# Two-block decode attention: K and V of block B in 32 KB rows per partition, two slots each, P^T spread by TensorE

## The chip, the cores and the metric

The kernel runs on one core of a Trainium2 chip. The metric is device time in microseconds (us), the median of repeated executions. Engines are called PE (TensorE), PEld (its weight loads), DVE (VectorE), ACT (ScalarE), POOL (GpSimd) and SP (SyncE, which here issues nearly all DMAs). Sixteen DMA engines move the data.

## The reference

Two blocks, A and B, do the same thing for one new token and are concatenated. A looks at the last 2048 cached positions, B at all 8192.

```python
# x: (1, 1, 576); k_cache, v_cache: (1, 16 heads, 8192, 128); wq: (576, 4096); wo: (4096, 576); bf16
q = (x @ wq).reshape(B, Sq, 32, 128).transpose(0, 2, 1, 3)
k = jnp.repeat(k_cache, 2, axis=1)      # A: positions Sk - 2048 .. Sk only
v = jnp.repeat(v_cache, 2, axis=1)
scores = jnp.einsum("bhqd,bhkd->bhqk", q, k) * (128 ** -0.5)
p = softmax(scores)
o = jnp.einsum("bhqk,bhkd->bhqd", p, v)
out = o.transpose(0, 2, 1, 3).reshape(B, Sq, 4096) @ wo
# result: concatenate([A's out, B's out])
```

Each K and V head of B is 8192 x 128 x 2 bytes = 2 MB, of A's window 0.5 MB. With wq and wo of both blocks 102.8 MB have to come from HBM once, and every byte is used for little arithmetic.

## The kernel before, in words

**Tiling.** K and V are loaded in groups of 8 MB: one group for A (all 16 heads, 2048 positions) and four for B (8 heads and 4096 positions each; groups 1 and 2 are the first 4096 positions, groups 3 and 4 the last). A group lies in four slots of 2 MB: `kslots` and `vslots` have NS = 4 slots of 8192 bf16 per partition. One load fills one slot: a partition receives TS = 64 consecutive positions of one head, one contiguous row of 16 KB; a slot holds four heads of A or two heads of B (`load_kv`, from L387). wq comes in pieces of 4, 4 and 1 units of 2048 columns (16, 16 and 4 KB per partition) into slots that K or V need later; wo comes in nine pieces.

**K rounds** (g = 0 to 4). PE transposes a slot's 64 blocks of 128x128 into PSUM in two units (`k_transpose`, L466; a unit is 4 banks of 8 blocks). Per unit ACT copies banks 0 and 2 to SBUF (L472) and DVE banks 1 and 3 (L475), into one of four `kt` buffers. `k_scores` (L486) multiplies the transposed unit with the queries of the slot's heads (`qst`, which POOL copies from `qtm`, L457) into the score tile `sacc`, 128x1024 in two PSUM banks. The stationary operand is zero in all rows but those of its heads, so units of all heads add into one tile, and the tile must be zero beforehand (`scores_zero`, L497, by PE).

**Softmax.** After rounds 0, 2 and 4 a chunk of scores is complete (A; B's first and second half). DVE masks (A only, L514) and takes the maximum (L515), ACT takes the exponential into `psb` (L523), writing each value twice. In the next odd round PE transposes `psb` (16 blocks, L536) and DVE writes it with a mask per parity of heads into `ptm` (L545, four operations).

**V.** At the end of rounds 1, 3, 4, 5 and 6 PE multiplies `ptm` with the four V slots of a group (`v_slot`, L557, 64 matmuls per slot) into `opsum`; DVE picks the valid part of each row (`v_keep`, L566 and L373). Round 6 also has the softmax weights of both blocks (`weights`, `combine`). Then come wo of A and of B (L646), a cast (L652) and a store (L658) each.

**What sets the order.** The program is a list of operations per engine, in order; `Program` derives semaphore waits from what each reads and writes. PE runs its rounds in a loop: an inner part (transposes, scores, in odd rounds P^T) and an outer part (V). Places in the loop are the numbers given as `loop=`. SP issues loads in the order of the list. It waits before a load until the last reader of the slot is done: PE's transposes for K slots, PE's V products for V slots. All loads of SP run on one queue, q1, first in first out.

Of the kernel before, what the change touches and what calls it, by code (L numbers as in the profile page):

```python
# [16 lines left out]
SLOT = 8192  # L17
UNIT = 4096
NS = 4
NKT = 4  # L20
TS = 64
WQ_UNITS = 9
WQ_U = 2048
OUTW = DM // 4
NEG = -1.0e30
# [13 lines left out]
class Program:  # L39
# [15 lines left out]
    def add(self, eng, fn, reads=(), writes=(), dma=None, after=(), tag=None, inc=1, loop=None):  # L55
        op = Op(eng, fn, tuple(reads), tuple(writes), dma, tag, 16 if dma is not None else inc, loop)
# [77 lines left out]
    def waits_of_loop(self, ops):  # L134
# [9 lines left out]
        for key, places in points.items():  # L144
# [26 lines left out]
            if len(fixed) == len(places):  # L171
                for place, hi in fixed.items():
# [4 lines left out]
                   for n in (1, 2, 16) for first in (0, n) if fits(first, n, some, taker)]  # L177
# [92 lines left out]
def bass_concat_heads__sliding_block_cached__gqa_block_cached__decode_kernel(  # L270
# [22 lines left out]
    G = [4, 2]  # L293
    CHUNK = [0, 1, 1, 2, 2]
    KIND = [0, 1, 2, 1, 2]
    base = [SK - W_A, 0]

# [3 lines left out]
    kslots = nc.alloc_sbuf_tensor("kslots", [128, NS, SLOT], BF16)  # L301
    vslots = nc.alloc_sbuf_tensor("vslots", [128, NS, SLOT], BF16)
    kt = nc.alloc_sbuf_tensor("kt", [128, NKT, UNIT], BF16)
    ptm = nc.alloc_sbuf_tensor("ptm", [128, 2048], BF16)
    psb = nc.alloc_sbuf_tensor("psb", [128, 2048], BF16)
# [6 lines left out]
    zero = nc.alloc_sbuf_tensor("zero", [128, 512], BF16)  # L312
    qtm = nc.alloc_sbuf_tensor("qtm", [128, 3 * 256], BF16)
    qst = nc.alloc_sbuf_tensor("qst", [128, NS * 64], BF16)
    xtwo = nc.alloc_sbuf_tensor("xtwo", [128, 2, 8], BF16)
    xpad = nc.alloc_sbuf_tensor("xpad", [128, 2, 10, 32], BF16)
    par2 = nc.alloc_sbuf_tensor("par2", [128, 2], F32)
    rows = nc.alloc_sbuf_tensor("rows", [128, 3, NS], F32)
# [4 lines left out]
    diag = nc.alloc_sbuf_tensor("diag", [128, 2, DH, NS], F32)  # L323
    acc = nc.alloc_sbuf_tensor("acc", [128, 7, DH], F32)
# [26 lines left out]
    def setup(pool):  # L351
        for t in (ident, xpad, selq, zero, warm, qtm, identf, same, pick):
            pool.memset(t[:], 0.0)
        pool.memset(onesf[:], 1.0)
        return pool.memset(opj[:], 0.0)

    add("pool", setup, writes=["ident", ("xpad", 0), ("xpad", 1), "selq", "ones", "warm", "zero", "identf", "pick", "same",
                               ("qtm", 0), ("qtm", 1), ("qtm", 2), ("opj", 0), ("opj", 1)])
# [9 lines left out]
    add("pool", select(identf[:], 0, [[-1, 128]], 1), reads=["identf"], writes=["identf"])  # L368
    for j in range(4):
        add("pool", select(pick[:], -128 * j, [[1, 4], [-1, 128]], 4), reads=["pick"], writes=["pick"])  # L370
# [8 lines left out]
    def load(dst, src, writes, dma, after=()):  # L379
        add("sp", lambda sp: sp.dma_start(dst, src()), writes=writes, dma=dma, after=after)  # L380

    def load_wq(P, k, dst, n, res):
        lo = 4 * k * WQ_U
        load(dst, lambda: wqs[P].rearrange("(m r) n -> m (r n)", m=64)
             .rearrange("m (e y) -> (m e) y", e=2)[:, lo:lo + n * WQ_U], [res], "wq%d%d" % (P, k))

    def load_kv(arrs, g, s, slots, name, after=()):  # L387
        P = 0 if g == 0 else 1
        i = s if g == 0 else 4 * ((g - 1) % 2) + s
        ch = 128 // G[P] * TS  # L390
        r0 = base[P] + (0 if g == 0 else (g - 1) // 2 * ch)

        def src():
            return arrs[P][0, i * G[P]:(i + 1) * G[P], r0:r0 + ch, :].rearrange("g (p t) d -> p g (t d)", t=TS)
        load(slots[:, s, :], src, [(name, s)], "%s%d" % (name, s), after)
# [3 lines left out]
    ODD = lambda g: (g & 1) == 1  # L399
    V_OF = {1: 0, 3: 1, 4: 2, 5: 3, 6: 4}  # L400
# [4 lines left out]
    prog.rounds_of, prog.outer = rounds_of, len(V_OF)  # L405
# [11 lines left out]
    def q_part(P, k, n, src, res):  # L417
        def mm(pe):
            for u in range(4 * k, 4 * k + n):
                for c in range(2):  # L420
                    for j in range(4):
                        n_ = 2 * j + c
                        x = u // 2 if n_ // 4 == u % 2 else 5 + (u + 1) // 2
                        o = (u - 4 * k) * WQ_U + (n_ % 4) * 512
                        ins = pe.matmul(qps[c][32 * j:32 * j + 32, :], lhsT=xpad[:, P, x, :],  # L425
                                        rhs=src[:, o:o + 512], start=(u == 0), stop=(u == WQ_UNITS - 1))
            return ins
        add("pe", mm, reads=[("xpad", P), res], writes=qbank)

    def q_finish(P):  # L430
# [12 lines left out]

        def put(dve):
            for e in range(2):
                if P == 0:
                    dst = bass.AP(tensor=qtm, offset=e, ap=[[768, 128], [4, 2], [34, 2], [72, 4]])
                else:
                    dst = bass.AP(tensor=qtm, offset=256 + e, ap=[[768, 128], [68, 2], [34, 2], [136, 4]])
                src = opsum[:, 0:32].rearrange("p (b a e j) -> p b a e j", b=2, a=2, e=2)[:, :, :, e, :]  # L450
                ins = dve.tensor_copy(dst, src)
            return ins
        add("dve", put, reads=[B_O], writes=[("qtm", 0)] if P == 0 else [("qtm", 1), ("qtm", 2)])

    def q_stage(g, s):
        o = KIND[g] * 256 + s * 64
        add("pool", lambda pool: pool.tensor_copy(qst[:, s * 64:(s + 1) * 64], qtm[:, o:o + 64]),  # L457
            reads=[("qtm", KIND[g])], writes=[("qst", s)], tag="q%d" % s)

    def k_transpose(g, u, place):  # L460
        s, half = divmod(u, 2)
        for q in range(4):
            def tr(pe, q=q):
                for t in range(8):
                    o = (32 * half + 8 * q + t) * 128
                    ins = pe.matmul(ktps_bf[q][:, t * 128:(t + 1) * 128], lhsT=kslots[:, s, o:o + 128],  # L466
                                    rhs=ident[:, :], start=True, stop=True, is_transpose=True)
                return ins
            add("pe", tr, reads=[("k", s), "ident"], writes=[("bank", q)], loop=(g, place + q / 8, K_ON, "inner"))
            dst = kt[:, u % NKT, q * 1024:(q + 1) * 1024]  # L470
# [8 lines left out]
    def k_scores(g, u, place):  # L479
        s, half = divmod(u, 2)  # L480

        def mm(pe):
            for e in range(2):
                for j in range(4):
                    rhs = kt[:, u % NKT, j * 1024:(j + 1) * 1024].rearrange("d (x g) -> d x g", g=2)[:, :, e]
                    ins = pe.matmul(sacc[32 * j:32 * j + 32, 512 * half:512 * half + 512],  # L486
                                    lhsT=qst[:, s * 64 + e * 32:s * 64 + e * 32 + 32],
                                    rhs=rhs, start=False, stop=True, skip_group_check=True)
            return ins
        add("pe", mm, reads=[("qst", s)] + [("kt", u % NKT, q) for q in range(4)], writes=[B_S[half]],  # L490
            loop=(g, place, K_ON, "inner"))

    def scores_zero(loop):
        for h in range(2):
            def mm(pe, h=h):
                for j in range(4):
                    ins = pe.matmul(sacc[32 * j:32 * j + 32, 512 * h:512 * h + 512], lhsT=zero[:, 0:32], rhs=zero[:, :],  # L497
                                    start=True, stop=True, skip_group_check=True)
                return ins
            add("pe", mm, reads=["zero"], writes=[B_S[h]], loop=loop and (loop[0], loop[1] + h / 8) + loop[2:])  # L500
# [7 lines left out]
    def softmax_exp(c):  # L508
        P, k = (0, 0) if c == 0 else (1, c - 1)
        if P == 0:  # L510

            v = sacc[:, :].rearrange("p (x b) -> p x b", b=2)
            m = bass.AP(tensor=maskS, offset=2, ap=[[4, 128], [0, 512], [1, 2]])
# [4 lines left out]
            reads=[("st", P, C_M + k)], writes=[("st", P, C_NB + k)])  # L518


        def go(act):
            src = bass.AP(tensor=sacc, offset=0, ap=[[1024, 128], [1, 1024], [0, 2]])
            return act.activation(psb[:, :].rearrange("p (x g) -> p x g", g=2), src, ACT.Exp, bias=st(P, C_NB + k),  # L523
                                  scale=SCALE, accum_out=st(P, C_L + k))
        add("act", go, reads=B_S + [("st", P, C_NB + k)], writes=["psb", ("st", P, C_L + k)], tag="exp")


    def softmax_transpose(g, place):
        for u in range(2):
            dst = (misc if u == 0 else opsum)[:, :].bitcast(BF16)  # L530
            bank = B_M if u == 0 else B_O

            def tr(pe, u=u, dst=dst):
                for t in range(8):
                    o = (8 * u + t) * 128
                    ins = pe.matmul(dst[:, t * 128:(t + 1) * 128], lhsT=psb[:, o:o + 128], rhs=ident[:, :],  # L536
                                    start=True, stop=True, is_transpose=True)
                return ins
            add("pe", tr, reads=["psb", "ident"], writes=[bank], loop=(g, place + u / 8, ODD, "inner"))

            def put(dve, u=u, dst=dst):
                for e in range(2):
                    to = ptm[:, u * 1024:(u + 1) * 1024].rearrange("p (n e y) -> p n e y", e=2, y=2)[:, :, e, :]
                    src = dst.rearrange("p (n e y) -> p n e y", e=2, y=2)[:, :, e, :]
                    ins = dve.tensor_scalar(to, src, par2[:, e:e + 1], None, ALU.mult)  # L545
                return ins
            add("dve", put, reads=[bank, "par2"], writes=[("ptm", u)], tag="put%d" % u, inc=1 if g == 1 else 2)


    def v_slot(vg, s, place, g):  # L550
        def mm(pe):
            for u in range(2):
                for t in range(8):
                    for j in range(4):
                        b = 32 * u + 8 * j + t
                        o = (u * 32 + t * 4 + j) * 32
# [199 lines left out]
```

## Time and profile before

| What | Value |
|---|---|
| median of three runs | 250.0 us (249.79 to 250.01) |
| profiled execution, its own time | 249.46 us |
| its span | 247.7 us |
| mean granted TensorE clock | 0.82 |
| bytes on SP's queue | 102.77 MB |
| steady rate, 30 to 220 us | 428 GB/s |
| ACT / DVE copies of K (L472 / L475) | 77.9 / 55.2 us |
| PE transposes of K (L466) | 85.1 us |
| V products (L557) | 28.1 us |

The profile gives, for each engine, busy time and share of the span; a table of 40 slices of the span with busy tenths of each engine, the TensorE clock that was granted, the DMA engines' busy share and their rate; the DMA queues with packets and bytes; the chain of work that ended last; groups of instructions by line with shapes, count, mean duration, and what ended the idle time before them. The trace behind it has every instruction, DMA packet (start, duration, size) and landing of a DMA (sixteen semaphore updates, one per DMA engine). "First" and "last landing" below are the first and the sixteenth of these.

### The profile page before, as it was taken

Reading aid. Unit: us, or ns where it says so; the run is one execution under the profiler, and the core shown is the slowest. Engines: PE = TensorE matmul, PEld = TensorE weight load, DVE = VectorE, ACT = ScalarE, POOL = GpSimd, SP = SyncE. Lnnn points to the kernel's source line nnn. Section 1 sums busy time; section 2 is a strip of 40 time slices with the busy share of each in tenths; the row PEclk is TensorE's granted clock in tenths of the full one; section 3 lists DMA queues with packets and bytes.
Section 4 is the critical chain, followed back from the end, with each engine's and each line's share of the span. In section 5 each row is a group of like instructions: output and inputs, shape, how many; then the busy total and the mean of one; then the engine's idle time right before and its main releaser. Section 6 shows DMA issues by size and latency. Waiting matters only on the chain. (4 is left out here: it accounts for less than half of the span.)

```text
span 247.7 us, 7505 instructions
## 1 busy us (share of the span) xinstructions
PE 169.6 (68%) x3406; PEld 132.3 (53%) x3406; DVE 81.0 (33%) x152; ACT 87.1 (35%) x92; POOL 12.9 (5%) x49
## 2 busy tenths in 40 slices
PE   0193589994999559995999638998345144685634
PEld 0031288763877458864878428785244142584522
DVE  0001225554555017564555122655004004204000
ACT  2000047767478009786578004775200000000000
POOL 7501000000000000000000000000000000000000
PEclk9999959999799979998899955999858755557555
DMA  7999999999999999999999999999999999999993
GB/s 270 406 433 431 430 431 421 426 423 429 431 425 429 426 421 431 422 431 434 423 429 429 423 431 429 426 437 426 429 429 423 431 426 429 434 427 427 421 406 138
DMA packets 8235, 102.92 MB, mean 416 GB/s; under 512 B 1184, under 2 KB 1312, under 8 KB 2080
## 3 DMA queue, kind: packets, MB, share of 16 engines
q1 hardware_dynamic: 7936, 102.77, 98.0%
q8 instruction: 8, 0.13, 0.2%
q10 hardware_dynamic: 288, 0.00, 0.1%
q14 instruction: 3, 0.02, 0.0%
HBM read 102.76 MB, written 0.00 MB: 415 GB/s over the span
## 5 line engine op out<-in xcount | busy, mean ns | idle before, releaser
L472 ACT ACTIVATE kt<-ktps 128x1024 bf16<-128x1024 bf16 x80 | 77.9, 1021 | 54.5 <-PE ktps L466 54.4
L466 PEld LDWEIGHTS ktps<-ident,kslots 128*128 128x128 bf16 x1280 | 78.9, 103 | 27.9 <-issue 27.9
L466 PE MATMUL ktps<-ident,kslots 128*128 128x128 bf16 x1280 | 85.1, 230 | 12.4 <-PEq L214 12.4
L475 DVE COPY kt<-ktps 128x1024 bf16<-128x1024 bf16 x80 | 55.2, 691 | 53.7 <-PE ktps L466 53.6
L557 PE MATMUL opsum<-vslots,ptm 128*32 128x128 bf16 x1280 | 28.1, 262 | 28.0 <-PEq L214 23.7
L557 PEld LDWEIGHTS opsum<-vslots,ptm 128*32 128x32 bf16 x1280 | 25.3, 119 | 31.6 <-issue 31.6
L486 PE MATMUL sacc<-kt,qst 128*32 128x512 bf16 x320 | 25.3, 392 | 1.8 <-PEq L214 1.8
L566 DVE TENSOR_TENSOR diag<-opsum,rows 128x512 f32<-128x512 f32 x5 | 3.5, 691 | 55.9 <-PE opsum L557 55.9
L425 PE MATMUL opsum<-vslots,xpad 128*32 128x512 bf16 x64 | 8.2, 489 | 14.8 <-DVE xpad L410 12.1
L599 ACT ACTIVATE stat<-stat 128x1 f32<-128x1 f32 (+1 forms) x2 | 0.6, 294 | 37.2 <-DVE stat L597 37.2
L425 PEld LDWEIGHTS opsum<-vslots,xpad 128*32 128x32 bf16 x64 | 2.3, 119 | 17.6 <-issue 13.1
L457 POOL COPY qst<-qtm 128x64 bf16<-128x64 bf16 x20 | 4.5, 236 | 123.2 <-PE sacc L486 113.5
L646 PE MATMUL ktps<-kslots,opj 128*32 128x144 bf16 x184 | 6.1, 326 | 5.8 <-DMA kslots<-in_B_wo_dram 3.9
L486 PEld LDWEIGHTS sacc<-kt,qst 128*32 128x32 bf16 x320 | 5.1, 94 | 8.2 <-issue 4.4
L431 ACT ACTIVATE qrow<-opsum 128x512 bf16<-128x512 f32 x2 | 1.2, 597 | 23.1 <-PE misc L425 23.1
L523 ACT ACTIVATE psb<-sacc,stat 128x2048 bf16<-128x2048 f32 x3 | 5.9, 1967 | 8.5 <-DVE stat L517 8.5
L646 PEld LDWEIGHTS ktps<-kslots,opj 128*32 128x32 bf16 x184 | 5.2, 145 | 6.4 <-DMA kslots<-in_B_wo_dram 4.2
L425 PE MATMUL misc<-vslots,xpad 128*32 128x512 bf16 x64 | 8.2, 487 | 0.0
L630 PE MATMUL misc<-acc,pick 128*128 128x32 f32 x16 | 3.8, 404 | 3.6 <-DVE acc L624 2.9
L433 DVE CAST qrow<-misc 128x512 bf16<-128x512 f32 x2 | 1.4, 692 | 14.6 <-PE misc L425 14.6
L652 DVE CAST outsb<-ktps 128x144 bf16<-128x144 f32 x2 | 0.6, 307 | 16.0 <-PE ktps L646 16.0
L630 PEld LDWEIGHTS misc<-acc,pick 128*128 128x128 f32 x16 | 3.6, 328 | 3.8 <-DVE acc L624 3.0
(66 smaller groups left out, 62.1 us busy)
## 6 DMA issues: line engine op xcount, KB each, us to landing
kslots<-in_B_k_cache_dram SPq DMA_DIRECT2D x16, 2048.0 KB, 19.6
vslots<-in_B_v_cache_dram SPq DMA_DIRECT2D x16, 2048.0 KB, 18.4
kslots<-in_A_k_cache_dram SPq DMA_DIRECT2D x4, 2048.0 KB, 29.8
vslots<-in_A_v_cache_dram SPq DMA_DIRECT2D x4, 2048.0 KB, 23.5
vslots<-in_A_wq_dram SPq DMA_DIRECT2D x2, 2048.0 KB, 9.9
vslots<-in_B_wq_dram SPq DMA_DIRECT2D x2, 2048.0 KB, 19.6
kslots<-in_A_wo_dram SPq DMA_DIRECT2D x2, 2016.0 KB, 23.8
kslots<-in_B_wo_dram SPq DMA_DIRECT2D x1, 2016.0 KB, 31.2
```

The costliest lines, as they stand in the source:

```text
L425: ins = pe.matmul(qps[c][32 * j:32 * j + 32, :], lhsT=xpad[:, P, x, :], rhs=src[:, o:o + 512], start=(u == 0), stop=(u == WQ_UNITS - 1))
L433: add("dve", lambda dve: dve.tensor_copy(qrow[:, 512:1024], misc[:, :]), reads=[B_M], writes=[("qrow", 1)])
L457: add("pool", lambda pool: pool.tensor_copy(qst[:, s * 64:(s + 1) * 64], qtm[:, o:o + 64]), reads=[("qtm", KIND[g])], writes=[("qst", s)], ...
L466: ins = pe.matmul(ktps_bf[q][:, t * 128:(t + 1) * 128], lhsT=kslots[:, s, o:o + 128], rhs=ident[:, :], start=True, stop=True, is_transpose ...
L472: add("act", lambda act, q=q, dst=dst: act.activation(dst, ktps_bf[q], ACT.Copy), reads=[("bank", q)], writes=[("kt", u % NKT, q)], tag="e ...
L475: add("dve", lambda dve, q=q, dst=dst: dve.tensor_copy(dst, ktps_bf[q]), reads=[("bank", q)], writes=[("kt", u % NKT, q)], tag="e%d%d" % ( ...
L486: ins = pe.matmul(sacc[32 * j:32 * j + 32, 512 * half:512 * half + 512], lhsT=qst[:, s * 64 + e * 32:s * 64 + e * 32 + 32], rhs=rhs, start ...
L523: return act.activation(psb[:, :].rearrange("p (x g) -> p x g", g=2), src, ACT.Exp, bias=st(P, C_NB + k), scale=SCALE, accum_out=st(P, C_L ...
L557: ins = pe.matmul(opsum[32 * j:32 * j + 32, s * DH:(s + 1) * DH], lhsT=ptm[:, o:o + 32], rhs=vslots[:, s, b * 128:(b + 1) * 128], start=(u ...
L566: return dve.tensor_tensor(diag[:, g % 2, :, :], opsum[:, :].rearrange("p (s d) -> p d s", s=NS), m, ALU.mult)
L630: ins = pe.matmul(misc[:, 0:32], lhsT=pick[:, r, :], rhs=acc[:, d, 32 * r:32 * r + 32], start=(r == 0), stop=(r == 3))
L646: ins = pe.matmul(ktps[P][32 * j:32 * j + 32, 0:OUTW], lhsT=opj[:, P, jj:jj + 32], rhs=view[:, o:o + OUTW], start=(jj == 0), stop=(jj == H ...
```

## The change

Five things change together.

- **Slots.** K has two slots of 16384 bf16 per partition and V has two. A load of B brings four heads of 4096 positions: 128 positions of one head per partition, one row of 32 KB, 4 MB in all. A's loads keep rows of 64 positions (16 KB), two loads to a slot. K, V and wq lie in one tile `kv`; wq of A is one load of 36 KB rows, wq of B two loads (20 and 16 KB), at the end of K's second slot and in V's.
- **Order of loads.** K, K, V per round instead of four K and then four V per group; wo's first piece has a tile of its own and is issued ahead of the V loads of group 3; the other seven wo pieces follow the last V load.
- **K rounds.** Eight units again, but four transposes come before the first scores, and scores are taken for two units at a time: for each of NG = 4 heads and 4 column groups one matmul, reading every fourth column of `kt`.
- **P^T.** The exponential is written once (1024 columns). After the odd round's scores PE transposes 8 blocks, DVE copies them to `pt0`, and PE multiplies with four constant 0/1 matrices `spread` (each repeats 32 of the 128 transposed rows four times) in eight matmuls of 512 columns, alternating between two PSUM banks; DVE multiplies each result with a head mask into `ptm` (now 4096 columns).
- **Smaller ones.** Scores are zeroed by a DVE memset behind the exponential, in place of PE's zero matmuls. `v_keep` is two DVE operations of 128 columns in place of two over 512. The factor 2 in the weights goes with the double writing.

The core of the diff:

```diff
-SLOT = 8192
+SLOT = 16384
-NS = 4
+NS = 2
+NG = 4
...
+    def load_kv(arrs, i, slots, name, after=()):
+        g, s = divmod(i, NS)
+        if g == 0:
+            for h in range(2):
+                def src(h=h):
+                    return arrs[0][0, 8 * s + 4 * h:8 * s + 4 * h + 4, base[0]:base[0] + W_A, :] \
+                        .rearrange("g (p t) d -> p g (t d)", t=64)
+                load(slots[s][:, h * 8192:(h + 1) * 8192], src, [(name, s, h)], "%s%d" % (name, s), after)
+        else:
+            h0 = 8 * ((g - 1) % 2) + 4 * s
+            r0 = (g - 1) // 2 * 4096
+
+            def src():
+                return arrs[1][0, h0:h0 + 4, r0:r0 + 4096, :].rearrange("g (p t) d -> p g (t d)", t=128)
+            load(slots[s], src, [(name, s, 0), (name, s, 1)], "%s%d" % (name, s), after, 2)
...
+        def mm(pe):
+            for g in range(NG):
                 for j in range(4):
+                    o = k0 * UNIT + j * 2048
+                    rhs = kt[:, o:o + 2048].rearrange("d (x g) -> d x g", g=NG)[:, :, g]
+                    o = ((2 * s + h) * NG + g) * 32
+                    ins = pe.matmul(sacc[32 * j:32 * j + 32, 512 * h:512 * h + 512], lhsT=qst[:, o:o + 32],
                                     rhs=rhs, start=False, stop=True, skip_group_check=True)
...
+        if c < 2:
+            add("act", lambda act: act.activation(warm[:, 4:8], warm[:, 0:4], ACT.Copy), reads=["warm"], writes=["tick"],
+                tag="tick")
+            scores_zero()
...
+        add("pe", tr, reads=["psb", "ident"], writes=[B_M], loop=(g, place, ODD, "inner"))
+        add("dve", lambda dve: dve.tensor_copy(pt0[:, :], misc[:, :].bitcast(BF16)), reads=[B_M], writes=["pt0"],
+            tag="pt0")
+        for k in range(8):
+            h, i = divmod(k, 4)
+            dst, bank = ((opsum, B_O), (misc, B_M))[k % 2]
+            add("pe", lambda pe, h=h, i=i, dst=dst: pe.matmul(dst[:, :], lhsT=spread[:, i, :],
+                                                              rhs=pt0[:, h * 512:(h + 1) * 512], start=True, stop=True),
+                reads=["pt0", "spread"], writes=[bank], loop=(g, place + (1 + k) / 16, ODD, "inner"))
+
+            def put(dve, h=h, i=i, dst=dst):
+                to = ptm[:, :].rearrange("p (h f i n y) -> p h f i n y", h=2, f=4, i=4, n=4)[:, h, :, i]
+                m = bass.AP(tensor=hmask, offset=0, ap=[[32, 128], [0, 4], [0, 4], [1, 32]])
+                return dve.tensor_tensor(to, dst[:, :].rearrange("p (f n y) -> p f n y", f=4, n=4), m, ALU.mult)
+            add("dve", put, reads=[bank, "hmask"], writes=[("ptm", k)], tag="put%d" % k, inc=1 if g == 1 else 2)
...
+        for lo, n in ([(0, 9)], [(0, 5), (5, 4)])[P]:
+            load_wq(P, lo, n, view[:, lo * WQ_U:(lo + n) * WQ_U], ("wq", P, lo))
+            q_part(P, lo, n, view, ("wq", P, lo))
...
+    order = ["k0 k1 v0", "k2 k3 v1", "k4 k5 v2", "k6 k7 v3", "k8 k9 v4 v5", "w0 v6 v7", "v8 v9 w1 w2 w3 w4 w5 w6 w7"]
...
     for g in range(7):
+        load_more(g)
         if g < 5:
             for s in range(NS):
                 q_stage(g, s)
+            for u in range(4):
+                k_transpose(g, u, u)
+            k_scores(g, 0, 6)
+            k_transpose(g, 4, 7)
+            k_transpose(g, 5, 8)
+            k_scores(g, 1, 9)
+            k_transpose(g, 6, 10)
+            k_transpose(g, 7, 11)
+            k_scores(g, 2, 12)
+            k_scores(g, 3, 13)
         if g % 2 == 1:
+            softmax_transpose(g, 14)
```

In what follows k0 to k9, v0 to v9 and w0 to w7 are the changed kernel's loads of K, V and wo by this list (k0, k1, v0 and v1 are A's, of two loads each), and T0 to T7 the eight units that a K round transposes.

## The prediction

> **What bounds the kernel now.** I read the page from the top: engines, slices, DMA queues, chain.
>
> ```profile
> span 247.7 us, 7505 instructions
> ...
> PE 169.6 (68%) x3406; PEld 132.3 (53%) x3406; DVE 81.0 (33%) x152; ACT 87.1 (35%) x92; POOL 12.9 (5%) x49
> ...
> DMA  7999999999999999999999999999999999999993
> ...
> q1 hardware_dynamic: 7936, 102.77, 98.0%
> ```
>
> No engine is full, but SP's queue (q1) is busy from the first slice to the last, 98% of sixteen DMA engines. The chain of waits in order of time ends so:
>
> ```profile
> 220.75 23.73 DMA vslots<-in_B_wo_dram
> 244.48 0.04 issue
> 244.52 0.71 PE ktps L646 x12
> 245.23 0.02 issue
> 245.26 0.31 DVE outsb L652
> ```
>
> The last wo pieces had been issued by 221.66 and landed only at 244.5 to 244.9, behind what the queue already held. So the end is the end of one unbroken stream, plus 2.8 us (matmuls, cast, store). Two things can move it: the stream's length, and whether SP always issues before the queue runs out. SP's own waits show that second thing is alive:
>
> ```profile
> SPq L380 <- PE ktps L466: 88.3, 15, 15.1
> SPq L380 <- PE opsum L557: 74.1, 14, 26.1
> ```
>
> SP waits for transposes (K slots) and V products (V slots). I call the time from an issue to the end of the stream already queued its slack; before, the smallest is about 6 us (issue 38.48; the load ahead of it first lands at 44.56).
>
> **The stream's length.** The landing records give the time between one load's first landing and the next one's, eight rows per DMA engine plus one small semaphore packet:
>
> ```
> row, bytes   us per load   8 rows at 0.036822 ns/B   rest, ns
> 16384        4.894         4.826                     68
> 16128        4.819         4.751                     68
>  9216        2.799         2.715                     84
>  4608        1.426         1.357                     69
>  3456        1.067         1.018                     49
> ```
>
> The slope comes from the 16128 and 4608 rows: 3.393 us over 92,160 B. So a load costs about 68 ns beside its bytes (7.6 ns for each of nine packets), whatever the row size. The diff moves the same bytes in fewer loads, still of eight rows per engine: K and V of B 32 to 16, wq of A 3 to 1, wq of B 3 to 2, wo 9 to 8; A's K and V stay at eight loads of 16 KB rows. That is 55 to 35, 20 x 68 ns = **1.36 us less**. Bounds: median packet records are 614 ns for 16384 B and 51 ns for 1152 B; against the slope they hold 9 to 11 ns each, and 160 rows and 20 semaphore packets at 12 ns are 2.1 us. From below it is 0.2 us, 20 semaphore packets at their recorded 9 ns, if a 32 KB row runs as two 16 KB ones. I take 1.36, the row of the loads concerned.
>
> The largest row in this trace is 16,384 B, so the slope of a 32 or 36 KB row is an extrapolation. What speaks for it: the five sizes lie on one line. Another unknown is the address pattern: a load of B now takes four heads 2 MB apart instead of two. A's loads do that already, and their landings lie 4.89 us apart like B's.
>
> [...]
>
> **Does the queue stay fed?** Half as many slots, each twice as large, mean that a refill asks for 4 MB of work to be finished first. I laid the new order on the stream (9.72 us for 4 MB, 9.79 for A's; last landing 1.9 us after the first, as throughout this trace).
>
> Engine costs. Four units of transposes in a row: 64 took 4.05 us at 91.83 (2.02 per unit of 32), so 8.1; from a cold clock 10.5, since 64 took 6.53 at 31.91, where the granted clock was 0.66. The rest of a K round alternates pairs of 3.9 (L466, 1.96 per unit) with 16 scores at about 1.0 (two times 0.63, overlapping): T7 ends 9.8 after T3, the scores 2.2 later. Scores now read every fourth column instead of every second: between no change and 1.7 (L425's cold 0.43 per group of four); I take 1.0, the nearest row. 128 V products: 2.0 warm (172 took 2.61), 3.6 cold (192 took 5.31).
>
> P^T is the new block, at the end of rounds 1, 3 and 5, in front of V on PE. Eight transposes 0.55 (16 took 1.06), a copy of 128x1024 0.69 (L475), a first spread of 0.39 (L486's mean), then eight DVE products over 512 f32 columns in PSUM. These have no row; L566, the same operation and size, takes 0.69; L545 takes 0.48 per 512, and L514's whole 1024 columns 1.23, which bound it. I take 0.69: with two PSUM banks the eight run on DVE one after another, 5.5 plus handovers, **7.6 us in all**, range 5.9 to 11.9. Queued behind it: V's products, then the next round. Off the path, and covered: the exp over 1024 instead of 2048 columns (-0.9 us of L523's 1.97), the DVE memset of the scores (0.6 to 1.3 by L566's and L514's sizes), which ends before the next K lands (next paragraph), v_keep's two 128-column operations (0.28 + 0.35 against 0.69 + 0.69), one more select on POOL (0.63).
>
> Slack then. The start first: wq of A now arrives in one piece, so its products begin near 14.6 instead of 11.4 and end near 20.5; k1, which waits for them, joins a stream that holds to 34.6. v0 waits for B's first piece, near 24.4: covered too. k2: round 0 starts when k0 has fully landed, 36.5, T3 47.0, the stream holds to 54.3: 7.3. Round 1 starts with k2 at 66.0: k4 7.0, k5 7; P^T ends 96.1, V of A's first slot 98.1, v2's slack **4.9**. Round 2 starts at once at 100.1: k6 at 108.2 against 112.7 (**4.5**), k7 at 118.0 against 122.4 (**4.4**); its memset is done by 124.4 (1.22 + 0.15 + 1.2 + 0.2 + 1.2 after the round's end at 120.2), and the next K lands at 124.3. Round 3 ends at 146.8, P^T 154.4, v4 4.8. Round 4 ends at 178.5, v6 5.0 thanks to w0 ahead of it. Last V slots: v6 landed 197.1, products cold 3.6, v8 4.2; v9 4.2. The first DMA of the run shows 1.0 us from issue (0.73) to the first packet (1.74), so about 3.2 us remain everywhere: no gap.
>
> **The end.** With w0 moved ahead of v6, the pieces behind V shrink from 22.2 us (220.76 to 242.99) to 17.4, and V lands later: v9 at 226.2, products until 229.8 (cold), v_keep and combine 2.1, L630 1.9, P = 0's 128 products 4.0 (72 took 2.35, 56 took 1.87): 237.9. P = 1's first piece then runs to 239.8; its last lands at 243.5. About 1 us is left, against 3.9 us of waiting (L646) before, so still the stream's end decides.
>
> **Sum.** The profiled execution took 249.46, its median sibling 250.0. 249.46 - 1.36 = 248.1; on the median's scale 250.0 - 1.36 = **248.6 us**.
>
> **Rivals.**
> - *Bigger rows bring nothing* (the cost goes with the bytes, or long rows are cut again): 0.2 us, 249.8. For it: no row over 16 KB in the trace. Against: the line above.
> - *The stream runs dry, slower.* Place: P^T in front of V and of round 2, at k6 and k7, then again at v4. It decides from 3.4 us more than I reckoned (4.4 less the 1.0 lead). At double price (1.38 per product) P^T grows by 5.5: 2.1 us of gap at k6/k7, 1.7 at v4 (4.8 less 1.0): 250.0 - 1.4 + 3.8 = 252.4. For it: the slack falls from 6 to 4.4 and P^T has no row. Against: 0.69 is measured on the same operation and size.
> - *PE becomes the end.* If products and projections stay cold and late by more than 1 us, one to two of it show: 249.0 to 250.2. Against: wo's pieces still land one after another.
> - The queue's last landing lags its first by 1.9 us and keeps doing so after eight 16 KB code packets (q8, 1.07 us each in the records) have joined the stream, presumably one per engine; a second one on the slowest engine would add 1 us. That is in the range, not a case of its own.
>
> **Numbers.** Forecast 0.60 (own range 247.9 to 249.4), nothing gained 0.12, dry stream 0.17, PE at the end 0.08, other 0.03. A measurement of this kernel tells about 0.2% (0.5 us) from no change. Faster: 0.60 and a little of PE's case, 0.62. Same: nothing gained and most of PE's case, 0.18. Slower: dry stream and the rest, 0.20. Range 247.8 (2.1 us saved) to 251.0 (a gap of 2.4 us).
>
> **What would show it.** q1's share and GB/s without a dip; 2,560 rows (20 loads x 128) and 320 semaphore packets fewer, so about 5,060 packets on q1; 4 MB loads of B landing 9.72 us apart instead of 9.79; DVE products of P^T near 0.69 us; issues of k6, k7, v4, v8 at least 3 us ahead of the stream's end. Wrong it is if 32 KB loads land 9.79 us apart or more, if a slice between 90 and 220 us shows DMA under 9 tenths, or if the last L646 no longer waits for a DMA.

## The result and the profile after

The changed kernel is slower. Its median is 259.6 us (256.8 to 260.2) against 250.0, a ratio of 1.0365 with a 95% interval of 1.0287 to 1.0442. The profiled execution took 260.13 us against 249.46, 10.7 us more. The forecast was 248.6 with a range up to 251.0. Here and below, medians and ranges are of all executions, and ratios leave out one slow execution (253.64 us, of the kernel with the permutation alone).

The same lines of the page as before, for the changed kernel:

```profile
span 258.1 us, 7455 instructions
...
PE 185.7 (72%) x3371; PEld 134.3 (52%) x3374; DVE 93.6 (36%) x174; ACT 82.8 (32%) x94; POOL 14.5 (6%) x40
...
DMA  7999999999999999858989999989996999999993
GB/s 286 446 403 420 427 427 432 422 465 414 422 420 437 434 442 424 361 253 325 366 366 467 427 406 457 437 330 442 432 401 259 406 442 452 406 416 437 426 405 115
...
q1 hardware_dynamic: 5056, 102.77, 94.3%
```

The bytes are the same and the packets 2,880 fewer, as counted beforehand. But the row of nines is broken: from the seventeenth slice (6.45 us each, so from 103 us) to the thirty-first the DMA engines have holes, and q1's share falls from 98.0% to 94.3%. The chain still ends on the stream:

```profile
225.08 29.86 DMA kv<-in_B_wo_dram
254.94 0.04 issue
254.99 0.70 PE ktps L655 x9
```

The wo piece that it names had been issued at 225 and waited 30 us behind the others, as before. So the loss lies earlier, where the queue was empty. SP's timeline shows which loads came late (start, duration, load):

```profile
101.67 0.55 SPq L388 DMA_DIRECT2D kv<-in_B_v_cache_dram  x1
116.27 11.83 SPq L388 DMA_DIRECT2D kv<-in_B_k_cache_dram  x2
128.14 0.60 SPq L388 DMA_DIRECT2D kv<-in_B_v_cache_dram  x1
...
167.39 3.23 SPq L388 DMA_DIRECT2D kv<-in_B_v_cache_dram  x2
...
195.04 27.37 SPq L388 DMA_DIRECT2D kv<-in_B_v_cache_dram  x4
```

These are v2; k6 and, at the end of that piece, k7 at 127.55; v3; v4 and v5; v6 to v9. The packet records give the holes to the microsecond. I add the time in which fewer than 16 packets were under way, as a share of 16 engines, and, in the last column, by how much the first packets behind the hole took longer than their size asks (bytes x 0.036822 ns + 9 ns; the excess of all packets, divided by the 16 engines):

```
hole, us           lost, us   slow packets behind it, us   load that ended it
102.62 - 103.20    0.26       0.50                         v2, issued 101.67
113.42 - 117.71    3.78       0.83                         k6, issued 116.27
128.15 - 129.40    0.91       0.58                         k7, issued 127.55
168.48 - 169.51    0.56       0.62                         v4, issued 167.39
193.78 - 196.97    2.61       0.54                         v6, issued 195.04
sum                8.12       3.07
```

With the 1.36 us that the shorter stream saves, this makes 8.1 + 3.1 - 1.4 = 9.8 of the 10.7 us. The other 0.8 I could not assign. In the windows view of the changed kernel (busy us per engine, granted clock, DMA share, GB/s) the largest hole looks so:

```profile
112.00:118.00 6.00, 6.00 (x91) 4.44 (x88) 3.87 (x6) 4.87 (x6) 0.00 (x0) 1.00 0.59 193
...
193.00:197.00 4.00, 3.41 (x235) 3.27 (x230) 1.38 (x2) 1.21 (x2) 0.00 (x0) 1.00 0.59 195
```

While the stream is down to 59%, PE is busy for the whole stretch (6.00 of 6.00 us): it is still transposing what must be gone before the next load may start. This is the path from round 1 to that load, on PE:

```profile
75.20 1.98 PE L506 MATMUL sacc<-kt,qst 128*32 128x512 bf16 x16
77.11 3.79 PE L481 MATMUL ktps<-ident,kv 128*128 128x128 bf16 x64
80.83 1.99 PE L506 MATMUL sacc<-kt,qst 128*32 128x512 bf16 x16
82.76 3.79 PE L481 MATMUL ktps<-ident,kv 128*128 128x128 bf16 x64
86.48 3.78 PE L506 MATMUL sacc<-kt,qst 128*32 128x512 bf16 x32
90.20 0.62 PE L545 MATMUL misc<-ident,psb 128*128 128x128 bf16 x8
91.91 0.38 PE L554 MATMUL misc<-pt,spread 128*128 128x512 bf16 x1 [1.09 <-PEq L214]
```

```profile
98.03 3.60 PE L571 MATMUL opsum<-kv,ptm 128*32 128x128 bf16 x128 [1.24 <-PEq L214]
101.85 1.79 PE L571 MATMUL opsum<-kv,ptm 128*32 128x128 bf16 x59 [0.22 <-PEq L214]
105.50 1.18 PE L571 MATMUL opsum<-kv,ptm 128*32 128x128 bf16 x69 [1.86 <-issue]
107.23 1.01 PE L481 MATMUL ktps<-ident,kv 128*128 128x128 bf16 x8 [0.55 <-PEq L214]
```

Two suspects stand out. Sixteen scores take 1.98 us where I had reckoned 1.0. And from the last score (90.3) to the first V product (98.03) PE goes at the pace of DVE's eight products of P^T (0.69 us each); from 93.6 on the granted clock is 0.5, and V then runs slowly (128 products in 3.60 us).

### The profile page after: what moved, and what is told of

Its sections match the earlier page's. It is cut to its first block, busy times and chain, and to the rows that moved or that the text cites. A ratio compares the mean times of both kernels' runs of the same rounds, so it can differ in the third digit from the quotient of the medians.

```text
span 258.1 us, 7455 instructions
## 1 busy us (share of the span) xinstructions
PE 185.7 (72%) x3371; PEld 134.3 (52%) x3374; DVE 93.6 (36%) x174; ACT 82.8 (32%) x94; POOL 14.5 (6%) x40
## 3 DMA queue, kind: packets, MB, share of 16 engines
q1 hardware_dynamic: 5056, 102.77, 94.3%
## 5 line engine op out<-in xcount | busy, mean ns | idle before, releaser
L481 PEld LDWEIGHTS ktps<-ident,kv 128*128 128x128 bf16 x1280 | 78.1, 102 | 25.9 <-issue 25.6
L481 PE MATMUL ktps<-ident,kv 128*128 128x128 bf16 x1280 | 81.3, 227 | 14.1 <-PEq L214 13.2
L571 PE MATMUL opsum<-kv,ptm 128*32 128x128 bf16 x1280 | 29.4, 273 | 16.5 <-PEq L214 14.7
L506 PE MATMUL sacc<-kt,qst 128*32 128x512 bf16 x320 | 38.9, 628 | 0.0
L571 PEld LDWEIGHTS opsum<-kv,ptm 128*32 128x32 bf16 x1280 | 27.3, 126 | 20.0 <-issue 20.0
L439 PE MATMUL opsum<-kv,xpad 128*32 128x512 bf16 x72 | 8.9, 471 | 17.2 <-DVE xpad L424 17.2
L655 PE MATMUL ktps<-kv,opj 128*32 128x144 bf16 x200 | 6.7, 296 | 4.0 <-DMA kv<-in_B_wo_dram 3.5
L561 DVE TENSOR_TENSOR ptm<-opsum,hmask 128x512 bf16<-128x512 f32 x12 | 8.3, 691 | 1.8 <-PE misc L545 1.8
L439 PE MATMUL misc<-kv,xpad 128*32 128x512 bf16 x72 | 8.8, 464 | 0.0
L561 DVE TENSOR_TENSOR ptm<-misc,hmask 128x512 bf16<-128x512 f32 x12 | 8.2, 686 | 0.5
```

The costliest lines, as they stand in the source:

```text
L561: return dve.tensor_tensor(to, dst[:, :].rearrange("p (f n y) -> p f n y", f=4, n=4), m, ALU.mult)
L571: ins = pe.matmul(opsum[32 * j:32 * j + 32, s * DH:(s + 1) * DH], lhsT=ptm[:, o:o + 32], rhs=vslots[s][:, b * 128:(b + 1) * 128], start=(m ...
L655: ins = pe.matmul(ktps[P][32 * j:32 * j + 32, 0:OUTW], lhsT=opj[:, P, jj:jj + 32], rhs=view[:, o:o + OUTW], start=(jj == 0), stop=(jj == H ...
```

## Experiments

Theory: PE's path between two refills became too long in two places, the scores that read every fourth column and P^T as a block in front of V. Rivals: only one of the two matters; the coarse 4 MB slots starve the stream whatever PE does; 32 KB rows bring nothing. Beside each set of runs the kernel before ran on the same chip; it took 250.2 us there. The changed kernel itself was not measured again beside these runs; beside its 259.6 us the kernel before took 250.0.

**Scores from runs of 32 columns.** The transposes of K multiply with a permutation matrix `perm` (1 at row 4x + g, column 32g + x) in place of the identity. It costs nothing on PE (64 transposes take 3.79 us with either matrix) and puts each head's 32 columns side by side.

```diff
+    add("pool", select(perm[:].rearrange("p (g x) -> p g x", g=NG), 0, [[-1, NG], [-4, 32]], 1), ...)
...
-                                    rhs=ident[:, :], start=True, stop=True, is_transpose=True)
+                                    rhs=perm[:, :], start=True, stop=True, is_transpose=True)
...
-                    rhs = kt[:, o:o + 2048].rearrange("d (x g) -> d x g", g=NG)[:, :, g]
+                    rhs = kt[:, o:o + 2048].rearrange("d (t g x) -> d g t x", g=NG, x=32)[:, g]
```

> The changed kernel with one part undone: the transposes of K multiply with a permutation matrix in place of the identity, so that the 32 columns of each head lie side by side in the transposed buffer and the scores read runs of 32 columns instead of every fourth. My theory: every fourth column halves PE's reading; 16 scores fall from 1.98 us to about 1.0, a K round by 3.5 us, k6 is issued near 112.5 instead of 116.3, its gap falls from 3.8 us to about 1, the others (k7 0.9, v4 0.6, v6 2.6) vanish: about 250.2 us. Rival 'four heads make the scores slow, not the stride': 16 scores stay at 1.98 and the time at 259.6. Rival 'it is P^T in front of V that starves the stream': scores fall, gaps at k6 and v6 stay over 2 us, about 255 us. Rival 'slots of 4 MB starve it whatever PE does': as that one.

Measured: 252.3 us (249.9 to 253.6 in ten runs), ratio 1.0068 (1.0041 to 1.0094). On the timeline the scores are those of the kernel before per matmul:

```profile
75.96 1.05 PE L509 MATMUL sacc<-kt,qst 128*32 128x512 bf16 x16
...
85.37 2.05 PE L509 MATMUL sacc<-kt,qst 128*32 128x512 bf16 x32
```

16 scores take 1.05 us instead of 1.98, so the stride is the cause and not the number of heads. Two holes remain, 0.31 us between v2 and k6 (issued 112.23) and 0.32 at k7; v4 and v6 have none. This one part is worth 7.3 of the 9.4 us of medians. The profiled execution took 251.99; its holes (0.6 us) and slow packets behind them (1.3) explain most of the distance to the kernel without holes below. So k6's hole fell further than I expected, and my 250.2 us was still 2 us too low: I had priced neither k7's hole nor the slow packets behind the two.

**P^T within the K round.** The eight transposes stand behind T2, the eight spread matmuls in four pairs behind the first scores, T5, T6 and the third scores. The work is the same. (The diff is abridged: S0 to S3 are the four groups of scores.)

```diff
-        if g % 2 == 1:
-            softmax_transpose(g, 14)
+        steps = [T0, T1, T2, None, T3, S0, None, T4, T5, None, S1, T6, None, T7, S2, None, S3]
+        # None: the next piece of P^T, in odd rounds, at places 2.5, 6.5, 8.5, 10.5, 12.5
```

> The changed kernel with the other suspect undone: in odd rounds P^T stands no longer behind the scores but in four pairs of spread matmuls between the transposes and scores of the K round, so that DVE's products (8 of 0.69 us) run beside PE's work; scores still read every fourth column. My theory: the 7.8 us between the last scores and V go, V runs at the full clock (2.0 us for 128 products instead of 3.6), v2 is issued near 95 and k6 near 107 instead of 116.3: no gap, 248.6 to 249.5 us. Rival 'stride alone decides': gaps at k6 and v6 stay over 1.5 us, over 253 us. Rival 'DVE becomes the limit in odd rounds (17 us of DVE in 24)': K rounds 1 and 3 grow by 4 us or more and the gain is halved, about 254 us.

Measured: 249.9 us (249.3 to 252.9 in ten runs), ratio 1.0001 (0.9977 to 1.0025). DVE's products take 688 and 683 ns, as in the changed kernel, but mostly hide: K round 1 with all of P^T in it lasts from 66.7 to 93.0, 2.3 us longer than without P^T (24.0) and not the 4 of the rival, and ends 5.0 us before the changed kernel's P^T (98.0). V follows at once, 128 products in 1.98 us instead of 3.60:

```profile
91.06 1.98 PE L506 MATMUL sacc<-kt,qst 128*32 128x512 bf16 x16
92.85 1.98 PE L574 MATMUL opsum<-kv,ptm 128*32 128x128 bf16 x128
```

v2 is issued at 94.9, k6 at 110.8, and one hole of 0.37 us remains, at k7. So the place of P^T is worth 9.7 us by itself, while the scores still read every fourth column. Both theories of a single cause fall: either edit alone removes most of the loss, because both lengthen the same path and what counts is by how much its sum passes the slack. The profiled execution was the slowest of the ten; one DMA engine ended 3.5 us behind the first there instead of 2, which I can't explain.

**Both.**

> Both: permutation matrix for K's transposes and P^T within the K round. My theory: no gap anywhere, q1 full from start to end, 248.6 us (1.4 less than before), K rounds of about 20 us. Rival '4 MB slots starve the stream whatever PE does': gaps over 1 us stay between 90 and 200 us, over 251 us. Rival 'rows of 32 KB bring nothing': no gap, and 249.8 to 250.0 us.

Measured: 249.2 us (249.1 to 249.2), ratio 0.9956 (0.9939 to 0.9972); a repetition gave 249.1, 0.9961 (0.9947 to 0.9975).

> The kernel with permutation and P^T within the round once more, beside the one with wq in three pieces and against the kernel before: 1.0 us less than before, ratio 0.996, as in its first run (249.2 against 250.23).

The page of the kernel with both parts has its nines back:

```profile
DMA  7999999999999999999999999999999999999993
...
q1 hardware_dynamic: 5056, 102.77, 97.5%
```

No hole of more than 0.1 us is in the packet records between 3 and 240 us, in either run. With the holes the loss is gone, so they were its cause, and this version is 0.4% faster than the kernel before. It is 0.6 us above the forecast, though its stream is full. Against the kernel before it saves 1.0 us, not 1.36.

**Row size alone.** As both, but each slot of B filled by two loads of 16 KB rows.

```diff
-            load(slots[s], src, [(name, s, 0), (name, s, 1)], "%s%d" % (name, s), after, 2)
+            for h in range(2):    # src(h): [:, :, h * 8192:(h + 1) * 8192]
+                load(slots[s][:, h * 8192:(h + 1) * 8192], src(h), [(name, s, h)], "%s%d" % (name, s), after)
```

> As the kernel with both, but each 4 MB slot of B filled by two loads of 16 KB rows (64 positions) instead of one of 32 KB rows; the slot is still freed as a whole. My theory: 16 loads more at 68 ns each, 1.1 us more than the kernel with both: 249.7 us; no gap. Rival 'the cost goes with the bytes, row size brings nothing': the same time as the kernel with both.

Measured: 250.3 us (250.0 to 250.6), ratio 1.0000 (0.9990 to 1.0009), no hole. In the windows view the stretch from 20 to 240 us of the kernel with 32 KB rows and of this one:

```profile
20.00:240.00 220.00, 157.40 (x3262) 129.19 (x3255) 91.56 (x170) 82.34 (x92) 3.97 (x10) 0.84 1.00 429
```

```profile
20.00:240.00 220.00, 156.16 (x3202) 128.15 (x3198) 91.25 (x169) 82.04 (x92) 3.97 (x10) 0.81 1.01 427
```

429 against 427 GB/s, and 1.06 us between the medians for sixteen loads: 66 ns per load, where 68 were reckoned. The median 32,768 B packet takes 1213 ns, two of 16,384 B take 1228. So the missing 0.3 us of the forecast is not in the row size: with 16 KB rows the new kernel should still have been 0.27 us faster than before (four loads fewer of wq and wo) and is not. Part of it shows at the end of the stream. In the profiles of the two runs with both parts the last wo load first lands at 242.12 and 241.68, 0.87 and 1.31 us earlier than before (242.99), but its last landing, at 244.21 and 244.14, is only 0.64 and 0.71 earlier (244.85): the slowest DMA engine trails by 2.1 and 2.5 us instead of 1.9. Why it does was not found.

**wq of A in three loads again**, in the kernel with both parts.

```diff
-        for lo, n in ([(0, 9)], [(0, 5), (5, 4)])[P]:
+        for lo, n in ([(0, 4), (4, 4), (8, 1)], [(0, 5), (5, 4)])[P]:
```

> The kernel with permutation and P^T within the round, but wq of A in three loads of 16, 16 and 4 KB rows instead of one of 36 KB rows. By 68 ns per load, 0.14 us more than the same kernel with one load; if its first products start earlier than with one load, that changes nothing, since k1 waits with 14 us to spare. Rival: the first piece in hand earlier shortens the start, and it is as fast or faster.

Measured: 249.4 us, ratio 0.9971 (0.9962 to 0.9981), beside 0.9961 (0.9947 to 0.9975) for the one load. The sign is the expected one, but the intervals overlap: not resolved.

**Slots in halves.** The changed kernel itself, with each slot filled, awaited and freed in halves.

```diff
-            add("pe", tr, reads=[("k", s, 0), ("k", s, 1), "ident"], ...)
+            add("pe", tr, reads=[("k", s, part // 2), "ident"], ...)
...
-    def v_slot(vg, s, place, g):        # for m in range(32)
+    def v_slot(vg, s, place, g, lo):    # for m in range(lo, lo + 16), reads ("v", s, lo // 16)
```

> The changed kernel (strided scores, P^T behind the scores) with slots filled, waited for and freed in halves of 2 MB, so rows of 16 KB: a K half is free after two units of transposes instead of four, a V half after 64 products instead of 128. If the coarse slots are a necessary part of the stall: the first half of k6 is issued about 4.3 us earlier (near 112 instead of 116.3), its gap falls under 0.5 us, v4's goes, v6's falls from 2.6 to about 1.3; with the 1.1 us that 16 KB rows cost, 251.5 to 253.5 us. Rival 'PE's longer path alone, slot size does not matter': gaps as before, 259 to 260 us.

Measured: 255.9 us (254.9 to 257.3), ratio 1.0248 (1.0209 to 1.0287), between the two theories. The trace shows why. The first half of k6 goes out at 107.74 and the holes at v2, k6 and k7 are gone; v4's has shrunk from 0.56 to about 0.2 us (near 162). But the one at v6 is larger, 3.7 us:

```profile
180.00:187.00 7.00, 7.00 (x96) 4.35 (x92) 2.92 (x5) 3.83 (x5) 0.00 (x0) 1.00 1.00 426
187.00:192.00 5.00, 4.89 (x208) 3.22 (x200) 1.38 (x2) 1.21 (x2) 0.00 (x0) 1.00 0.28 78
```

PE is busy nearly all the time (7.00 of 7.00 and 4.89 of 5.00 us). Round 4's scores end at 188.8 and the first half of V's products at 189.7; only then may the load go out. So 4 MB slots are a condition for the holes at k6 and k7 and for most of v4's, where a half is free some us earlier (k6's first load went out at 107.74 instead of 116.27). At v6 they are not: there PE as a whole is late, by the scores of five rounds and two blocks of P^T, and halves did not help. The runs above, with one of the two undone, have no hole at v6. The rival "slot size does not matter" falls, and my expected 1.3 us at v6 falls too: I had not seen that a stream without earlier holes arrives at v6 earlier.

**The clock behind P^T.** The changed kernel with two matmuls of 512 columns added behind each spread matmul; nothing reads their result.

```diff
+            def keep(pe):
+                for _ in range(2):
+                    ins = pe.matmul(ktps[0][:, :], lhsT=ident[:, :], rhs=pt0[:, 0:512], start=True, stop=True)
+                return ins
```

> The changed kernel with idle work added: behind each spread matmul of P^T PE does two matmuls of 512 columns into a free PSUM bank, whose result nobody reads, so that PE is busy while DVE works. If the dropped clock behind P^T is part of the loss: the granted clock stays at 1.0 after P^T, 128 V products take 2.0 us instead of 3.6 in rounds 1 and 3 and the transposes behind them 8.0 instead of 9.0; k6 is issued about 3 us earlier, its gap falls to about 0.7, v2's and v4's go, v6's falls to about 0.5: 251.5 to 253.5 us. Rival 'P^T's own 7.8 us do it, the clock does not matter': P^T and V as long as before, 259 to 260 us.

Measured: 259.3 us, ratio 1.0371 (1.0346 to 1.0396), no gain. The effect on the clock is there: between 93.6 and 103.8 us the granted clock (the third figure from the end; first the changed kernel, then this one) is 1.0 instead of 0.5, and 128 products take 1.97 us instead of 3.60:

```profile
93.60:103.80 10.20, 8.22 (x192) 5.33 (x191) 3.81 (x6) 0.00 (x0) 0.00 (x0) 0.50 0.99 410
```

```profile
93.60:103.80 10.20, 6.95 (x191) 4.22 (x189) 4.48 (x7) 0.00 (x0) 0.00 (x0) 1.00 0.98 416
```

```profile
98.59 1.97 PE L577 MATMUL opsum<-kv,ptm 128*32 128x128 bf16 x128 [0.81 <-PEq L214]
101.15 0.79 PE L577 MATMUL opsum<-kv,ptm 128*32 128x128 bf16 x43 [0.58 <-PEq L214]
105.19 2.53 PE L577 MATMUL opsum<-kv,ptm 128*32 128x128 bf16 x85 [3.25 <-issue]
107.81 7.79 PE L481 MATMUL ktps<-ident,kv 128*128 128x128 bf16 x128
```

But a pause that lasted 1.86 us in the changed kernel's profile lasts 3.25 here, the 85 products behind it run at the slow pace again (2.53 us), and the round began with 9.56 us of transposes instead of 9.00. So k6 goes out at 115.63, only 0.6 us earlier. What the faster V and the next transposes (7.79 against 9.00) save is taken back before it reaches a refill. Round 3 goes the same way: its 128 products fall from 3.61 to 1.97 us, but the granted clock is 0.5 from 135.9 to 139.3, where it was 1.0, and 88 of the round's first transposes take 6.73 us instead of 5.14; v6 goes out 0.5 us earlier.

```profile
135.47 6.73 PE L481 MATMUL ktps<-ident,kv 128*128 128x128 bf16 x88 [0.26 <-PEq L214]
```

My expected 252 us was wrong: keeping PE busy behind P^T moved the slow stretches in this profile and bought nothing. What a full clock throughout would be worth, no run shows; for the changed kernel's loss, the two edits above suffice without it.

## Why the prediction was wrong

- **What bounds the kernel, right.** The end is the end of one stream, and its two levers are its length and the refills. The chain after shows it as the chain before did.
- **The stream's length, right in the term, 0.3 us short in the sum.** 55 to 35 loads at 68 ns; the row size alone measured 66 ns per load. The extrapolation to 32 KB rows held, and the loads of four heads 2 MB apart cost no rate: 429 GB/s between 20 and 240 us with both parts, 427 in the kernel before. Of the 1.36 us, 1.0 was seen with a full stream. (The upper bound of 2.1 us took 12 ns per packet where the rows beside it had 9 to 11, which makes 1.6 to 2.0.)
- **"Slack then": the step that failed.** k6 was put at 108.2 and went out at 116.27. Term by term, against 66.0 + 10.5 + 12.0 + 7.6 + 4.0 + 8.1 = 108.2: round 1 began 0.3 later; T0 to T3 took 9.0 instead of 10.5 (-1.5); the rest of the round 15.0 instead of 12.0 (+3.0); P^T 7.8 instead of 7.6 (+0.2); V's two slots 8.65 instead of 4.0 (+4.65: 1.6 and 1.0 for the slow products of the first and second slot, 0.2 between the slots, 1.86 for a pause); 0.55 to the next round; its T0 to T3 9.0 instead of 8.1 (+0.9). The sum is +8.1. That T0 to T3 of round 1 took less than the 10.5 was luck; without it k6 would have been later still. (The memset's end in round 2, put at 124.4, is 124.2 by its own terms.)
- **The scores** were the term I named as unknown, "between no change and 1.7", and took at 1.0. The measured 1.98 us lies above my own upper end. A round's four groups took 7.75 us (1.98 + 1.99 + 3.78) where I had 4.2, which over five rounds is about 18 us of PE.
- **V "2.0 warm"** was wrong although I had the cold row, 3.6, beside it. P^T, as I described it, leaves PE waiting for DVE, and work behind a wait in the profile of before (31.91) came with a low granted clock (0.66 from 30 to 40 us). I should have taken the cold value there, or both.
- **The pause in V of round 1** was in the profile of before, 4.3 us against "issue" at L557, and I left it out.
- **P^T itself, right in size**: 690 ns per product where 690 was taken, 7.8 us where 7.6 was reckoned.
- **The rival "the stream runs dry" is what happened**, at k6, k7 and v4 as written, and at v6 and v2. Its price of 252.4 was too low, and its chance of 0.17 looks so: the price had one cause only (P^T at double price) and no cost for a restart, which came to 0.6 us each. With slacks of 4.2 to 5.0 us on a path of 42 us (66 to 108), resting on estimates of which two had no row of their own (P^T and the scores), "about 3.2 us remain everywhere: no gap" was too sure.
- **The end, right**: the last matmul still waits for a DMA. The late V made no difference.

## What to carry to other kernels

When a kernel lives on one unbroken stream of loads, an edit that shortens the stream by 1.4 us is worth that only as long as every refill is released in time; lay the new order on the stream, price each releasing path with its worst plausible rows (slow clock, pauses, unknown access patterns) and compare the sum with the slack, rather than the middle values. Larger slots make each release later by their own work: here k6 went out at 116.27, and with halves its first load at 107.74. A fix may cost little or nothing: here a permutation in place of the identity (64 transposes take 3.79 us with either) removed the strided read (16 scores take 1.05 us instead of 1.98), and a DVE-bound chain of 7.8 us, moved in between PE's work, made the round only 2.3 us longer.

## What the runs showed of the hardware

- The scores that read every fourth bf16 column (8 bytes apart) as moving operand ran at about half speed: 16 matmuls of 512 columns take 1.98 us, with runs of 32 columns 1.05. Groups of four concurrent ones (628 ns each) start 0.45 us apart (weight loads at 116.60 and 117.05 in the changed kernel). With every second column (before) 8 take 0.63 us.

```profile
116.17 0.12 PEld L506 LDWEIGHTS sacc<-kt,qst 128*32 128x32 bf16 x8
116.60 0.14 PEld L506 LDWEIGHTS sacc<-kt,qst 128*32 128x32 bf16 x4 [0.31 <-issue]
117.05 0.14 PEld L506 LDWEIGHTS sacc<-kt,qst 128*32 128x32 bf16 x4 [0.31 <-issue]
```

- In the changed kernel a hole in the stream cost more than its length: the packets behind each hole took longer than their size asks, by 0.5 to 0.8 us per DMA engine on average.
- PE's first pass through V's products, in round 1, has a pause of 4.31 us before, 1.86 in the changed kernel, 3.96 with both parts and 3.25 with the added matmuls. At the first three of these lies a packet of 16 KB (about 1.0 us) on q8, the queue that the profile lists as "instruction": from 86.70 to 87.77 before, where the pause runs from 84.89 to 89.20, from 102.91 to 103.99 in the changed kernel, where it runs from 103.64 to 105.50, and from 95.56 to 96.57 with both parts, where it runs from 94.17 to 98.13. Whether the packet causes the pause, no run shows.
- Packets of 32,768 B take 1213 ns, of 36,864 B 1364 ns in the changed kernel: on the line of the smaller ones (0.036822 ns per byte and 7 ns; there 16,128 B take 601 ns, 9,216 B 347).
